# Attention and two feed-forward stages on one core: an order written by a planner gets new ranks and new costs

## The chip, the core and the metric

The program runs on one core of one Trainium2 chip. The metric is the time in microseconds (us) of an execution on the device; lower is better.

## What is computed

The reference, cut to what matters:

```python
def phi(x):                                   # x: (4, 8, 576, 64)
    proj = einsum('bhsd,df->bhsf', x, w_phi)  # 64 -> 128 features
    proj = proj - max(abs(proj), axis=-1)
    return concatenate([exp(proj), exp(-proj)], axis=-1)
q_p, k_p = phi(q), phi(k)
kv = einsum('bhsf,bhsd->bhfd', k_p, v);  z = sum(k_p, axis=2)
attn = einsum('bhsf,bhfd->bhsd', q_p, kv) / (einsum('bhsf,bhf->bhs', q_p, z) + 1e-6)
x = heads side by side                        # (2304, 512)
x = max(x @ w1, x @ w2, x @ w3) @ w_out       # 512 -> 768 -> 512
xn = x / sqrt(mean(x * x) + 1e-6) * rms_g
out = (silu(xn @ w_gate) * (xn @ w_val)) @ w_out2   # 512 -> 1536 -> 512
```

## The kernel before

**Three stages.** Attention is done in eight units of two heads; a unit has 1152 columns, taken in three thirds of 384 columns. The first feed-forward stage and the second one go over five column tiles (384, 512, 512, 512 and 384 of the 2304 columns), six times and six times. A product of the feed-forward stages is three matmuls, since each operand is held as a rounded part and a rest.

**One third of attention.** On the k side: `k_proj` (TensorE, tile `pk`), `k_max` and `k_sub` (VectorE, tiles `mk` and `e`), two exponentials per head (ScalarE, `e`), `kv_sum` (TensorE, `pkv`), and once per unit a copy `kvs` (ScalarE). On the q side: `q_proj` (TensorE, `pq`), two copies `pc` (ScalarE), `q_max` (GpSimd, a partition all-reduce into `mq`), `q_sub` (VectorE, `pc`), two exponentials (ScalarE, `eq` and `pc`), `attend` (TensorE, `nd`), then on VectorE `guard`, `invert` (both `den`) and `divide` (`xs`), the transposes `turn` (TensorE, again in a `pq` bank), and the rounded part `xh` (ScalarE) and the rest `xl` (VectorE) of the columns for the next stage. The denominators come from columns of ones beside v in the tiles `vt` and `vm`.

**The weights.** A piece of weights (512 columns of a 64-bit load) is turned into a rounded part and a rest by one ScalarE magnitude, five VectorE steps (`narrow`, L622, L626, L630, L634 and L636), a ScalarE rounding and two subtractions or additions (L650 and L652). These two run on VectorE for the first four pieces, which are prepared while attention runs, and on GpSimd for all later ones. The first 384 and the next 512 columns of the first feed-forward stage (tile `first`) are multiplied while attention ends.

**What sets the order.** Nothing in the program is ordered by loops: every step is an entry of a `Planner` (a step's engine, its rank, its assumed time, what it reads and writes). `order()` plays the program with these assumed times, and takes on each engine, of the steps that could start within 0.12 us of the first, the one with the lowest rank. The engines then run their instructions in that order. The assumed times are constants (`act_us`, `dve_us`, `pool_us`, `HALF`, `KPROJ`, `ISSUE`, `LOAD`), `U` is the assumed length of a unit, and `A` the rank at which the first feed-forward stage begins. Buffers are rings of slots: a new tenant of a slot waits until the last step of the old one is done. The rings that matter below are in PSUM: `pk` has banks 0 and 1, `pq` has 2, 3 and 7, the results `po` of the feed-forward stages have 4 to 7, and the sums and the spread scale of the normalisation (`pn`, L786 and L793) have bank 7 as well. All loads and stores are issued by SyncE's queue, in the planner's order. Ahead of everything TensorE runs ten matmuls on ones (`wake`, L342).

Of the kernel before, what the change touches and what calls it, by code (L numbers as in the profile page):

```python
# [46 lines left out]
class Planner:  # L47
# [18 lines left out]
    LAG = {"PE": 0.25, "DVE": 0.2, "ACT": 0.15, "POOL": 0.1}  # L66

    def op(self, eng, rank, busy, fn, r=(), w=(), lag=None, size=0, after=(), kind=None, when=0.0):
        lag = self.LAG.get(eng, 0.0) if lag is None else lag
        self.ops.append(dict(eng=eng, rank=rank, busy=busy, fn=fn, r=tuple(r), w=tuple(w), lag=lag, size=size,  # L70
                             after=after, kind=kind, when=when, i=len(self.ops)))

    def order(self):
# [39 lines left out]
        cand = {}  # L113
# [30 lines left out]
        while done < len(ops):  # L144
            best = None
            for eng, c in cand.items():
                e0 = free.get(eng, 0.0)
                l = []
                for i in c:
                    p = place(ops[i])  # L150
                    if p is not None:
                        l.append((max(e0, ready[i], p[0]), i, p[1]))
                if l:
                    first = min(x[0] for x in l)
                    pick = min((x for x in l if x[0] <= first + 0.12), key=lambda x: (ops[x[1]]["rank"], x[1]))
# [4 lines left out]
            t, i, claims = best  # L160
# [13 lines left out]
            if o["size"]:  # L174
                dma_free = max(dma_free, t + 1.2) + o["size"] / 240e3
# [16 lines left out]
def act_us(n, psum=False):  # L192
    return n / 1200.0 + (0.06 if psum else 0.105)


def dve_us(n):
    return n / 960.0 + 0.075


def pool_us(n):  # L200
    return n * 0.00235 + 0.15


R384, R256, R512, FULL, HALF, KPROJ = 0.173, 0.118, 0.229, 0.222, 0.13, 1.1
ISSUE = 0.6
# [3 lines left out]
def attn_moe_kernel(ctx, tc, qT, kT, vv, w_phi, w1, w2, w3, wo1, wg, wv, wo2, rms_g, out):  # L209
# [108 lines left out]
    def load_phi():  # L318
        for r in halves:
            nc.sync.dma_start(out=wst[r, :], in_=w_phi)  # L320
# [11 lines left out]
    def fill_v(i):  # L332
        vt, vm = vts[i]
        nc.gpsimd.memset(vm, 0.0)
        for b in range(2):
            nc.gpsimd.memset(vm[b * D:(b + 1) * D, :, b, D:D + 1], 1.0)
        nc.gpsimd.memset(vt[:, :, :, D:D + 1], 1.0)

    pl.op("SP", -100, 2 * ISSUE, load_phi, w=["wphi"], size=1 << 16, lag=2.0)
    def wake():  # L340
        for _ in range(10):
# [3 lines left out]
    pl.op("PE", -101, 4.0, wake, r=["ones2"], w=[new("nd", "wake")])  # L345
    pl.op("DVE", -99, 0.3, clear, w=["ones", "eps"])
    pl.op("ACT", -98, 1.4, lambda: nc.scalar.activation(out=eps, in_=eps, func=ACTF.Copy), r=["eps"], w=["eps"])
    for i in range(2):
# [5 lines left out]
          w=["gsc"], size=1 << 14, lag=4.0)  # L354
# [10 lines left out]
    U = 17  # L365
    LOAD = 2.5

    def unit(n):
# [9 lines left out]
        def load_v(b):  # L378
            if b < 2:
                r = halves[b]  # L380
                nc.sync.dma_start(out=vm[r, :, b, 0:D], in_=vv[g, hp, r, MIX])
# [525 lines left out]
```

## Time and profile before

| | us |
|---|---|
| median of 3 runs | 895.05 |
| lowest and highest run | 894.75 and 895.14 |
| the profiled execution's own time | 894.96 |
| its span, first to last instruction | 893.3 |
| TensorE busy in the span | 881.5 |
| VectorE busy | 572.8 |
| ScalarE busy | 335.5 |
| GpSimd busy | 242.3 |

The profiled execution is 0.09 us below the median, and 1.7 us of its time lie outside the span. TensorE's busy time counts a matmul until its modelled end, so that pipelined matmuls overlap; what a stage costs is read from when the next group of matmuls starts.

### The profile page before, as it was taken

How to read it: one execution, taken by the hardware profiler on the slowest of the kernel's cores; microseconds unless marked ns; L12 is line 12 of the kernel's file. 1: busy time of each engine (PE TensorE's matmuls, PEld its weight loads, DVE VectorE, ACT ScalarE, POOL GpSimd, SP SyncE). 2: the span in 40 equal slices, each digit the busy share in tenths (PEclk: the TensorE clock that was granted, in tenths of full speed). 3: DMA queues.
4: the chain of work that ended last, by engine and by line, in shares of the span. 5: the costliest groups of instructions: out<-in, count | busy, mean ns of one | idle time of the engine just before them, and what ended most of it. 6: DMA issues, size and time to landing. Idle time of an engine off the chain costs nothing.

```text
span 893.3 us, 15539 instructions
## 1 busy us (share of the span) xinstructions
PE 881.5 (99%) x6434; PEld 766.8 (86%) x6434; DVE 572.8 (64%) x1004; ACT 335.5 (38%) x640; POOL 242.3 (27%) x161
## 2 busy tenths in 40 slices
PE   8998999999999999999999999999999999999998
PEld 7887888898989889898978888898898888889887
DVE  4799897678775859496887337367366555533323
ACT  5998995452212212124565432123123122211110
POOL 3455453353312312043441222024024022200000
PEclk9999999999999999999999999999999999999999
DMA  8544321232220302011011013012011101000112
GB/s 213 139 121 125 106 73 44 72 95 70 72 72 1 95 25 72 23 48 48 1 48 48 1 48 94 1 48 71 24 47 48 48 8 41 1 0 1 48 59 106
DMA packets 53973, 51.38 MB, mean 58 GB/s; under 512 B 21520, under 2 KB 49296, under 8 KB 53904
## 3 DMA queue, kind: packets, MB, share of 16 engines
q1 hardware_dynamic: 53904, 50.41, 18.8%
q8 instruction: 50, 0.82, 0.4%
q14 instruction: 19, 0.16, 0.1%
HBM read 45.68 MB, written 4.72 MB: 56 GB/s over the span
## 4 chain that ended last, share of the span: by engine, by line
PE 89%; DVE 4%; POOL 3%; issue 2%; ACT 1%; POOLq 0%; ACTq 0%
PE up L361 56%; PE po L361 25%; POOL mq L474 3%; PE nd L499 2%; PE first L361 2%; PE pkv L432 1%; PE pq L468 1%; DVE pc L481 1%; PE pk L400 1%; DVE mk L407 1%; PE nd L342 1%; DVE xs L510 0%; PE pn L786 0%; PE pq L518 0%; PE pkv L429 0%
## 5 line engine op out<-in xcount | busy, mean ns | idle before, releaser
L361 PE MATMUL up<-xh,wp 128*128 128x512 f32 (+1 forms) x1632 | 488.5, 368 | 0.0
L361 PEld LDWEIGHTS up<-xh,wp 128*128 128x128 f32 x1632 | 302.6, 188 | 39.5
L361 PE MATMUL up<-xl,wp 128*128 128x512 f32 (+1 forms) x816 | 300.2, 368 | 0.0
L650 POOL TENSOR_TENSOR wa<-wa,wp 128x512 f32<-128x512 f32 x56 | 78.0, 1393 | 396.7 <-ACT wp L644 313.6
L361 PEld LDWEIGHTS up<-xl,wp 128*128 128x128 f32 x816 | 153.2, 188 | 20.4
L725 ACT CAST hh<-hf 128x512 fp32r<-128x512 f32 (+1 forms) x90 | 52.2, 580 | 246.6 <-DVE hf L833 130.8
L833 DVE TENSOR_TENSOR hf<-up,hf 128x512 f32<-128x512 f32 (+1 forms) x60 | 38.1, 635 | 161.4 <-PE up L361 159.0
L694 DVE TENSOR_TENSOR acc<-po,acc 128x512 f32<-128x512 f32 (+1 forms) x190 | 122.8, 659 | 21.0 <-PE po L361 19.3
L361 PE MATMUL po<-wp,hh 128*128 128x512 f32 x432 | 133.5, 390 | 0.0
L361 PEld LDWEIGHTS po<-wp,hh 128*128 128x128 f32 x432 | 80.7, 188 | 15.8
L831 ACT ACTIVATE hf<-up 128x512 f32<-128x512 f32 (+1 forms) x60 | 33.4, 556 | 160.5 <-PE up L361 160.5
L474 POOL PARTITION_ALL_REDUCE mq<-pc x24 | 66.9, 2788 | 68.1 <-ACT pc L471 62.4
L361 PE MATMUL po<-wp,hl 128*128 128x512 f32 x216 | 84.5, 391 | 0.0
L652 POOL TENSOR_TENSOR wp<-wa,wm 128x512 fp32r<-128x512 f32 x56 | 78.5, 1401 | 9.0 <-DVE wm L636 5.0
L361 PE MATMUL po<-hh,wp 128*128 128x512 f32 (+1 forms) x240 | 79.1, 370 | 1.6 <-DVE acc L800 1.6
L726 DVE TENSOR_TENSOR hl<-hf,hh 128x512 fp32r<-128x512 f32 (+1 forms) x90 | 67.1, 746 | 15.7 <-ACT hh L725 15.6
L749 DVE TENSOR_TENSOR hf<-up,hf 128x512 f32<-128x512 f32 (+1 forms) x56 | 35.6, 635 | 62.0 <-PE up L361 62.0
L636 DVE SCALAR_TENSOR_TENSOR wm<-wst,wm 128x512 f32<-128x512 uint32 x60 | 54.4, 906 | 1.0
L361 PEld LDWEIGHTS po<-hh,wp 128*128 128x128 f32 x240 | 44.7, 188 | 7.9 <-issue 1.9
L419 ACT ACTIVATE e<-e 128x384 f32<-128x384 f32 x96 | 47.0, 535 | 8.7 <-DVE e L412 8.1
L615 ACT ACTIVATE wm<-wst 128x512 f32<-128x512 f32 x60 | 40.1, 671 | 22.9 <-POOL wp L652 18.0
L622 DVE TENSOR_SCALAR wm<-wm 128x512 f32<-128x512 f32 x60 | 32.5, 543 | 24.5 <-ACT wm L615 24.5
(74 smaller groups left out, 948.2 us busy)
## 6 DMA issues: line engine op xcount, KB each, us to landing
wst<-in_moe_w_dram SPq DMA_DIRECT2D x18, 512.0 KB, 3.5
wst<-in_moe_w_out_dram SPq DMA_DIRECT2D x18, 512.0 KB, 3.5
wst<-in_moe_w_gate_dram SPq DMA_DIRECT2D x12, 512.0 KB, 3.5
wst<-in_moe_w_val_dram SPq DMA_DIRECT2D x12, 512.0 KB, 3.5
kraw<-in_kT_dram SPq DMA_DIRECT2D x24, 192.0 KB, 3.4
qraw<-in_qT_dram SPq DMA_DIRECT2D x24, 192.0 KB, 2.6
out_dram<-acc SPq DMA_DIRECT2D x18, 256.0 KB, 2.0
vt<-in_vv_dram SPq DMA_DIRECT2D x16, 256.0 KB, 4.0
```

Of the source, the lines that this page charges most:

```text
L361: mm(out=ps, lhsT=a, rhs=b, start=start and i == 0, stop=stop and i == n - 1)
L419: nc.scalar.activation(out=dst, in_=src, func=ACTF.Exp, scale=-1.0 if u else 1.0)
L474: nc.gpsimd.partition_all_reduce(buf(f"mq{n}.{c}").rearrange("p a c -> p (a c)"), buf(f"pc{n}.{c}").rearrange("p a c -> p (a c)"), P, bass ...
L615: nc.scalar.activation(out=buf(f"wm{self.id}").bitcast(FP32), in_=self.view()[1].bitcast(FP32), func=ACTF.Abs)
L636: nc.vector.scalar_tensor_tensor(out=mf, in0=lo.bitcast(U32), scalar=2.0 ** -52, in1=mf, op0=ALU.mult, op1=ALU.mult)
L650: eng.tensor_tensor(out=a, in0=a, in1=r32(buf(self.h)), op=ALU.subtract)
L652: eng.tensor_tensor(out=buf(self.l), in0=a, in1=buf(f"wm{self.id}").bitcast(FP32), op=ALU.add)
L694: nc.vector.tensor_tensor(out=acc, in0=p, in1=acc, op=ALU.add)
L725: pl.op("ACT", rank, act_us(n), lambda: nc.scalar.copy(out=buf(h)[:, 0:n], in_=buf(f)[:, 0:n]), r=[f], w=[h])
L726: pl.op("DVE", rank + 0.6, dve_us(n) + 0.1, lambda: nc.vector.tensor_tensor(out=buf(l)[:, 0:n], in0=buf(f)[:, 0:n], in1=r32(buf(h)[:, 0:n] ...
L749: pl.op("DVE", b_at(m, t, q), dve_us(n), lambda f=f, p=p, n=n: nc.vector.tensor_tensor(out=buf(f)[:, 0:n], in0=buf(p)[:, 0:n], in1=buf(f)[ ...
L833: pl.op("DVE", g_at(m, t, q + 4.1), dve_us(n), lambda f=f, p=ups[1], n=n: nc.vector.tensor_tensor(out=buf(f)[:, 0:n], in0=buf(p)[:, 0:n], ...
```

## The change

The planner is given other assumed times; it counts a switch of TensorE between matmuls on half the rows, on half the columns and on the whole array (`form`, 0.13 us); and it holds back a step of VectorE or GpSimd that reads two operands from SBUF, or is one of the simple `narrow` steps, while the other engine holds the port that the two share (`lock`, `fast`). All ranks get other constants. No matmul is added or taken away but four of the ten ahead of everything. `w_phi` is loaded from ScalarE's queue, and SyncE's first loads get an order of their own (`FIRST`). v gets its ones in the first and last column of a row of 130, so that a load writes 128 elements in one piece where it wrote twice 64. The matmuls of v have the same shapes as before. The core of the diff:

```diff
-    def op(self, eng, rank, busy, fn, r=(), w=(), lag=None, size=0, after=(), kind=None, when=0.0):
+    LAG = {"PE": 0.24, "DVE": 0.12, "ACT": 0.14, "POOL": 0.09}
+    TURN = 0.13
+    def op(self, eng, rank, busy, fn, r=(), w=(), lag=None, size=0, after=(), kind=None, when=0.0, form="whole", lock=0.0, fast=0.0):
...
-                        l.append((max(e0, ready[i], p[0]), i, p[1]))
+                        t = max(e0, ready[i], p[0])
+                        if ops[i]["lock"]:
+                            lo, hi, far = held["POOL" if eng == "DVE" else "DVE"]
+                            hi = far if ops[i]["fast"] else hi
+                            t = hi if lo <= t < hi else t
+                        late = eng == "PE" and form != ops[i]["form"]
+                        l.append((t, i, p[1], t + 0.0 * late))
...
+            if o["lock"]:
+                held[o["eng"]] = (t, t + o["lock"], t + max(o["lock"], o["fast"]))
...
+            if o["eng"] == "PE" and form != o["form"]:
+                busy += self.TURN
+                form = o["form"]
...
-            pools["attnk"].tile([P, NST - 1, 2, D + 1], FP32, name=f"vt{i}"),
-            pools["attnk"].tile([P, 2, 2, D + 1], FP32, name=f"vm{i}"),
+            pools["attnk"].tile([P, NST - 1, 2 * D + 2], FP32, name=f"vt{i}"),
+            pools["attnk"].tile([P, 2, 2 * D + 2], FP32, name=f"vm{i}"),
...
-            nc.sync.dma_start(out=wst[r, :], in_=w_phi)
+            nc.scalar.dma_start(out=wst[r, :], in_=w_phi)
...
-        for _ in range(10):
+        for _ in range(6):
             mm(out=buf("wake")[:, 0:P], lhsT=ones2, rhs=ones2, start=True, stop=True)
...
-    U = 17
-    LOAD = 2.5
+    U = 16.67
+    LOAD = 0.4
+    FIRST = {b: i - 40.0 for i, b in enumerate(("k1", "k0", "k2", "q0", "q1", "v2", "v3", "v0", "v1"))}
+    FIRST["q2"] = 8.58
...
-            pl.op("POOL", rk - 8, 2.75, lambda c=c: q_max(c), r=[f"{pc}:0", f"{pc}:1"],
+            pl.op("POOL", rk - 7.67, 2.69, lambda c=c: q_max(c), lock=1.57, fast=2.62, r=[f"{pc}:0", f"{pc}:1"],
...
-    A = NU * U + 24.0
+    A = NU * U + 16.39
```

What the new plan makes of it, at three places. First SyncE's queue at the program's start: `kraw`, `qraw`, `vt` and `vm` are the raw k, q and v of a third, `wst` is `w_phi`. Before:

```order
L320 DMA wst_84<-in_w_phi_dram 64x128 x2
L376 DMA kraw_124<-in_kT_dram 128x384
L376 DMA kraw_127<-in_kT_dram 128x384
L376 DMA kraw_129<-in_kT_dram 128x384
L385 DMA vt0_91<-in_vv_dram 128x8x64
L381 DMA vm0_92<-in_vv_dram 64x2x64
L385 DMA vt0_91<-in_vv_dram 128x8x64
L464 DMA qraw_134<-in_qT_dram 128x384
```

After:

```order
L391 DMA kraw_117<-in_kT_dram 128x384
L391 DMA kraw_122<-in_kT_dram 128x384
L391 DMA kraw_125<-in_kT_dram 128x384
L480 DMA qraw_127<-in_qT_dram 128x384
L480 DMA qraw_129<-in_qT_dram 128x384
L400 DMA vt0_91<-in_vv_dram 128x4x128 x2
L396 DMA vm0_92<-in_vv_dram 64x128 x2
```

The two loads of `w_phi` have left this queue, and two thirds of q stand ahead of v; the k of the first third is now the second load.

Second, TensorE at the program's start, with the ten or six matmuls on ones first, then `k_proj` (`pk`), `q_proj` (`pq`) and `kv_sum` (`pkv`). Before, up to the first `kv_sum`:

```order
L342 MATMUL nd<-ones_90 128x128 x10
L400 MATMUL pk<-wst,kraw 128x128 x12
L432 MATMUL pkv<-vt_91,e_162 64x65 x2
L432 MATMUL pkv<-vt_91,e_156 64x65 x2
```

After:

```order
L354 MATMUL nd<-ones_90 128x128 x6
L415 MATMUL pk<-wst,kraw 128x128 x6
L484 MATMUL pq<-qraw,wst 128x384 x4
L415 MATMUL pk<-wst,kraw 128x128 x6
L448 MATMUL pkv<-vt_91,e_161 64x65 x2
L448 MATMUL pkv<-vt_91,e_153 64x65 x2
```

Two thirds of `q_proj` have moved ahead of the second `k_proj`; before, a `q_proj` stood behind the first `kv_sum` and ahead of the third `k_proj`, and there none stands now.

Third, VectorE where weight steps lie between the `q_sub` of a third (written to `pc`) and its `divide` (`xs`). Before, of the second piece (L626, L630, L634):

```order
L529 TENSOR_TENSOR xl_612<-pq,xh_609 128x192 x2
L626 TENSOR_SCALAR wm<-wm 128x512
L630 SCALAR_TENSOR_TENSOR wa<-wst,wm 128x512
L481 TENSOR_TENSOR pc<-pc,mq 128x768
L502 TENSOR_SCALAR den<-nd 128x6
L634 TENSOR_SCALAR wm<-wa 128x512
L507 RECIPROCAL den<-den 128x6
L407 TENSOR_REDUCE mk<-pk 128x3
L510 TENSOR_TENSOR xs<-nd,den 128x384
```

After, of the second piece as well (L645, L649 and L653 are the same three steps):

```order
L645 TENSOR_SCALAR wm<-wm 128x512
L518 TENSOR_SCALAR den<-nd 128x6
L497 TENSOR_TENSOR pc<-pc,mq 128x768
L523 RECIPROCAL den<-den 128x6
L649 SCALAR_TENSOR_TENSOR wa<-wst,wm 128x512
L526 TENSOR_TENSOR xs<-nd,den 128x384
```

The step that wrote `wa` has moved from ahead of the `q_sub` to behind it, and the third of the steps into the next third, right behind that third's `q_sub` and `guard`; only one step is left between a `guard` and its `divide`.

## Rows read from the trace of the kernel before

**Rows 1.** The page's first part: busy us, share of span, instructions.

```profile
PE 881.5 (99%) x6434; PEld 766.8 (86%) x6434; DVE 572.8 (64%) x1004; ACT 335.5 (38%) x640; POOL 242.3 (27%) x161
```

**Rows 2.** The chain that ended last, in order of time: start us, us, what.

```profile
206.23 5.48 PE up L361 x24
255.77 5.48 PE up L361 x24
...
528.02 5.44 PE up L361 x24
...
602.01 5.44 PE up L361 x24
```

**Rows 3.** The chain in attention: first and twentieth attend, three q_proj in a row.

```profile
23.22 1.42 PE nd L499 x48
...
116.53 0.84 PE pq L468 x4
...
121.47 0.84 PE pq L468 x4
...
125.28 1.55 PE nd L499 x48
126.83 0.84 PE pq L468 x4
```

**Rows 4.** TensorE's waits: total us, times, longest.

```profile
PE pq L518 <- DVE xs L510: 3.0, 3, 2.2
PE po L361 <- DVE acc L800: 1.6, 1, 1.6
```

**Rows 5.** Timeline of VectorE, then of GpSimd, 79 to 87 us.

```profile
80.86 1.36 DVE L626 TENSOR_SCALAR wm<-wm 128x512 int32<-128x512 int32 x1
...
82.86 0.95 DVE L481 TENSOR_TENSOR pc<-pc,mq 128x768 f32<-128x768 f32 x1
...
83.80 1.83 DVE L634 TENSOR_SCALAR wm<-wa 128x512 int32<-128x512 int32 x1
...
86.08 0.54 DVE L510 TENSOR_TENSOR xs<-nd,den 128x384 f32<-128x384 f32 x1
...
79.20 2.74 POOL L474 PARTITION_ALL_REDUCE mq<-pc  x1 [2.50 <-ACT pc L471]
83.34 3.25 POOL L474 PARTITION_ALL_REDUCE mq<-pc  x1 [1.40 <-ACT pc L471]
```

**Rows 6.** Stretches of 1 us: length, busy us by engine, granted clock, DMA.

```profile
10.00:11.00 1.00, 1.00 (x21) 1.00 (x22) 1.00 (x3) 0.31 (x1) 0.03 (x1) 0.50 0.80 253
...
88.00:89.00 1.00, 1.00 (x23) 1.00 (x20) 1.00 (x3) 0.95 (x3) 0.00 (x0) 0.50 0.06 16
```

**Rows 7.** The chain right behind the stall at 84 to 87 us.

```profile
87.08 2.12 PE nd L499 x48
89.20 1.58 PE pq L468 x4
90.78 0.95 PE pk L400 x12
```

**Rows 8.** The chain at the start, and one later kv_sum.

```profile
1.11 4.63 PE nd L342 x20
5.74 1.02 PE pk L400 x12
6.76 1.57 issue
8.33 0.46 PE pk L400 x2
...
10.01 2.80 PE pkv L432 x48
12.81 0.85 PE pq L468 x4
13.66 0.67 PE pk L400 x12
...
118.04 1.55 PE pkv L432 x48
```

**Rows 9.** SyncE's first k loads in the timeline; time to landing, 0 to 6 us.

```profile
2.04 1.53 SPq L376 DMA_DIRECT2D kraw<-in_kT_dram  x3
...
kraw<-in_kT_dram SPq DMA_DIRECT2D x3, 192.0 KB, 2.6
```

**Rows 10.** Timeline around the change of stage: TensorE and VectorE.

```profile
441.95 0.65 PE L793 MATMUL pn<-ident,rc 128*128 128x128 f32 x4
...
447.52 0.75 DVE L800 SCALAR_TENSOR_TENSOR acc<-acc,gsc,pn 128x512 f32<-128x512 f32 x1
...
448.42 0.47 PE L361 MATMUL po<-hh,wp 128*128 128x512 f32 x1 [1.65 <-DVE acc L800]
```

**Rows 11.** One normal step of each of two kinds, VectorE, 96 to 117 us.

```profile
107.33 0.39 DVE L622 TENSOR_SCALAR wm<-wm 128x512 f32<-128x512 f32 x1
...
112.62 0.65 DVE L630 SCALAR_TENSOR_TENSOR wa<-wst,wm 128x512 int32<-128x512 int32 x1
```

More of the change, by code (lines that the diff above doesn't have):

```diff
@@ L65 @@
     SWAP = 7.4
-    LAG = {"PE": 0.25, "DVE": 0.2, "ACT": 0.15, "POOL": 0.1}
-    def op(self, eng, rank, busy, fn, r=(), w=(), lag=None, size=0, after=(), kind=None, when=0.0):
+    LAG = {"PE": 0.24, "DVE": 0.12, "ACT": 0.14, "POOL": 0.09}
+    TURN = 0.13
+    def op(self, eng, rank, busy, fn, r=(), w=(), lag=None, size=0, after=(), kind=None, when=0.0, form="whole", lock=0.0, fast=0.0):
         lag = self.LAG.get(eng, 0.0) if lag is None else lag
         self.ops.append(dict(eng=eng, rank=rank, busy=busy, fn=fn, r=tuple(r), w=tuple(w), lag=lag, size=size,
-                             after=after, kind=kind, when=when, i=len(self.ops)))
+                             after=after, kind=kind, when=when, form=form, lock=lock, fast=fast, i=len(self.ops)))
     def order(self):
@@ L353, in attn_moe_kernel @@
     pl.op("SP", 20, ISSUE, lambda: nc.sync.dma_start(out=gsc, in_=rms_g.rearrange("(k p) -> p k", p=P)),
-          w=["gsc"], size=1 << 14, lag=4.0)
+          w=["gsc"], size=1 << 14, lag=4.0, when=60.0)
     def mm3(ps, terms, start=True, stop=True):
@@ L380, in load_v @@
                 r = halves[b]
-                nc.sync.dma_start(out=vm[r, :, b, 0:D], in_=vv[g, hp, r, MIX])
+                nc.sync.dma_start(out=vm[r, b, 1:2 * D + 1], in_=vv[g, hp, r, MIX].rearrange("p j d -> p (j d)"))
             else:
@@ L426, in kv_sum @@
                     first, last = t == 0 and u == 0, t == NST - 1 and u == 1
+                    head = slice(j * (D + 1), (j + 1) * (D + 1))
                     for r in halves:
                         if t == MIX:
-                            mm(out=ps[r, u], lhsT=e[:, r], rhs=vm[:, j], start=first, stop=last)
+                            mm(out=ps[r, u], lhsT=e[:, r], rhs=vm[:, :, head], start=first, stop=last)
                         else:
                             b = int(t > MIX)
-                            mm(out=ps[r, u, b, :], lhsT=e[:, r], rhs=vt[:, t - b, j, :], start=first, stop=last)
+                            mm(out=ps[r, u, b, :], lhsT=e[:, r], rhs=vt[:, t - b, head], start=first, stop=last)
         def kv_copy(j):
@@ L554, in unit @@
             for j in range(2):
-                pl.op("PE", rk + j, 6 * HALF, lambda c=c, j=j: attend(c, j),
+                pl.op("PE", rk - 0.47 + 0.57 * j, 6 * HALF, lambda c=c, j=j: attend(c, j), form="cols",
                       r=[eq, f"{pc}:0", f"{pc}:1", f"kvs{n}.{j}"], w=[f"{nd}:{j}"])
-            pl.op("DVE", rk + 2.0, 0.12, lambda c=c: guard(c), r=[f"{nd}:0", f"{nd}:1"], w=[den])
-            pl.op("DVE", rk + 2.1, 0.14, lambda c=c: invert(c), w=[den])
-            pl.op("DVE", rk + 2.2, dve_us(C), lambda c=c: divide(c), r=[f"{nd}:0", f"{nd}:1", den], w=[xs])
-            pl.op("PE", rk + 2.5, 0.3, lambda c=c: turn(c), r=["ident", xs], w=xt)
+            pl.op("DVE", rk + 2.76, 0.085, lambda c=c: guard(c), r=[f"{nd}:0", f"{nd}:1"], w=[den])
+            pl.op("DVE", rk + 2.76 + 0.1, 0.1, lambda c=c: invert(c), w=[den])
+            pl.op("DVE", rk + 2.76 + 0.2, dve_us(C), lambda c=c: divide(c), r=[f"{nd}:0", f"{nd}:1", den], w=[xs])
+            pl.op("PE", rk + 2.54, 0.16, lambda c=c: turn(c), form="rows", r=["ident", xs], w=xt)
             for h, part in [(h, part) for h in range(2) for part in parts(c, h)]:
@@ L663, in plan @@
             new("wp", self.l)
-            pl.op("SP", w, ISSUE, self.load, w=[st], size=P * 512 * 8, lag=LOAD, when=max(0.0, w - 20) if i < 4 else 0.0)
+            pl.op("SP", w, ISSUE, self.load, w=[st], size=P * 512 * 8, lag=LOAD, when=max(0.0, w - 20.0) if i < 4 else 0.0)
             if self.wide:
@@ L718, in fn @@
             mm3(buf(ps)[:, 0:CW[t]], [(wh[:, k * P:(k + 1) * P], wl[:, k * P:(k + 1) * P], h[:, k, :], l[:, k, :]) for k in range(KD)])
-        pl.op("PE", rank, 12 * mm_us(CW[t]), fn, r=xin(s, t) + [piece.h, piece.l], w=[ps], lag=0.3, when=EARLY)
+        pl.op("PE", rank, 12 * mm_us(CW[t]), fn, r=xin(s, t) + [piece.h, piece.l], w=[ps], lag=0.2, when=EARLY)
         return ps
@@ L743, in attn_moe_kernel @@
             early = "first" if m == 0 and C0[t] + n <= T else "up"
-            ups = [plan_up(b_at(m, t, q), 0, f"{key}.{i}", pieces1[m][i], t, early) for i, q in enumerate((0.0, 1.97, 4.92))]
+            ups = [plan_up(b_at(m, t, q), 0, f"{key}.{i}", pieces1[m][i], t, early) for i, q in enumerate((0.0, 0.31, 4.41))]
             f = new("hf", f"hf{key}")
```

126 lines of the change are left out of this document (65 added, 61 removed).

## Prediction

> **What bounds the kernel now.** I read the page's busy times first, then the chain of work that ended last, then TensorE's waits, and last the timeline where these waits lie. TensorE is busy for 99% of the span [rows 1], so the time is TensorE's work plus the stretches in which it waits or runs slowly. The chain shows that the two feed-forward stages hold no such stretch: one of the six rounds of the first stage takes 255.77 - 206.23 = 49.54 us, and one round of the second 602.01 - 528.02 = 73.99 us [rows 2]. Six of each are 297.2 + 443.9 = 741.1 us, and they are the same matmuls after the change. The other 893.3 - 741.1 = 152.2 us are the start, attention, the change of stage and the tail, and only there can time be won.
>
> In attention the reader is to see how dense TensorE is. Where nothing waits, a third takes 121.47 - 116.53 = 4.94 us, and the third of a unit that holds the mixed tile takes 126.83 - 121.47 = 5.36 us [rows 3]. From the first `attend` at 23.22 to the twentieth at 125.28 us there are 19 thirds, of which 6 are of the longer kind: dense they would be 13 x 4.94 + 6 x 5.36 = 96.4 us, and they took 102.1 us. So 5.7 us of this stretch are excess, and everything ahead of 23.22 us is the filling of the pipeline. The last thirds are filled up with `first` matmuls and show no wait.
>
> The waits name the places: TensorE waited three times for `xs` before `turn`, at the longest 2.2 us, and once 1.6 us in the feed-forward part for the scaled `acc` [rows 4]. The long one lies at 84 to 87 us. There the step L626 took 1.36 us, of which most went by until the all-reduce of 79.20 had ended at 81.94; `q_sub` could start only at 82.86; then L634, standing between `guard` and `invert`, took 1.83 us beside the next all-reduce, which began at 83.34, and so `divide` ended at 86.62 [rows 5]. A step of this shape takes 0.39 us when it has the port [rows 11]. Behind the stall TensorE's granted clock was 0.50 [rows 6], its lower level of 1.2 GHz: the next `attend`, `q_proj` and `k_proj` took 2.12, 1.58 and 0.95 us [rows 7], against 1.55, 0.84 [rows 3] and 0.67 [rows 8]. That is 0.57 + 0.74 + 0.28 = 1.6 us more. So one stall of this kind costs 2.2 + 1.6 = 3.8 us, two thirds of the excess.
>
> **The change, term by term.**
>
> *The start.* TensorE's first `k_proj` begins at 5.74 us, right when the ten matmuls on ones end; these take 4.63 us [rows 8]. Six take 0.6 of it and end near 3.9 us. SyncE issued the first k load at 2.04 us, with 0.5 us an issue, and it landed 2.6 us later [rows 9], so it was there before TensorE was. With `w_phi` on another queue SyncE starts with k, about 1.2 us earlier; the k that is needed is the second load now, so it lands near 2.04 - 1.2 + 0.5 + 2.6 = 3.9 us too. The first `k_proj` comes some 1.6 us earlier. Then the order differs. Before, the second `k_proj` waited until 8.33 for a free bank of `pk`; the first `kv_sum` followed at 10.01 and took 2.80 us at a granted clock of 0.50 [rows 6, 8], where 1.55 is usual; a `q_proj` of 0.85 us came next, and the third `k_proj` ran only at 13.66. After, four matmuls of `q_proj` fill the wait for the bank (1.7 us, or 3.2 us at the lower clock), and none stands ahead of the third `k_proj`: 0.85 us less, and 1.25 us less if the clock is up for `kv_sum`. The second `k_proj` then gains 0 to 1.5 us and the third 0.9 to 3. Since the first two `q_max` are begun early, `q_sub` is no longer what the first `attend` waits for; it inherits the gain of the k side. Bounds: 0 and -4 us; I take the middle of the third `k_proj`'s gain and the earlier q side, **-2.5 us**.
>
> *The thirds between.* Removed is the pattern of 84 to 87 us: the second piece's L630 stands behind `q_sub` and not ahead of it, and L634 is put into the next third, directly behind `q_sub` and `guard`, when an all-reduce has just ended. Steps ahead of `q_sub` still meet the all-reduce, but `q_sub` waits for that same all-reduce anyway, so they cost only their own 0.39 to 0.65 us [rows 11]. What stands between `guard` and `divide` is one such step, and TensorE has a `q_proj`, a `k_proj` and half a `kv_sum` (0.84 + 0.67 + 0.78 = 2.3 us) to do before `turn` asks for `xs`. Without the stall 5.7 - 3.8 = 1.9 us of excess stay, and I leave 0.2 for new small waits. Bounds: everything goes (-5.7), or a stall like it arises elsewhere (0). I take **-3.6 us**.
>
> *The change of stage.* The 1.65 us wait is one for a bank: a `po` result of bank 7 had to wait until VectorE had read the spread scale of L793 from that bank for the last time, 447.52 + 0.75 us, though the transposes were done at 442.6 [rows 10]. The new order again puts some 5 us of matmuls between such a transpose and the next use of bank 7, twice, where the need was 5.8 us. Bounds 0 and -1.65 us; I take **-0.4 us**.
>
> *Costed at nothing.* The new ranks of the feed-forward stages: the matmuls are the same, and a round has no wait to lose [rows 2]. Were a step late there, it would come back in every round. ScalarE's two issues of `w_phi`: it has nothing to do before the first `k_sub`, which follows the first `k_proj`; without this cover, 1.2 us. The layout of v: its loads go in fewer, longer pieces, which helps only the start, and is inside that term's bounds; matmuls, `guard` and `divide` keep their sizes. The last thirds: the order of `q_proj`, `first` and `attend` differs a little, and TensorE has 72 `first` matmuls to put into gaps as before.
>
> The sum is -2.5 - 3.6 - 0.4 = -6.5 us on the profiled execution's own 894.96 us: 888.5 us. The median of the runs is 0.09 us above that execution, so I forecast **888.5 us**.
>
> **Two rules beside the rows.** The row shows a granted clock of 0.50 in the stretch from 10 us on, after TensorE had waited from 6.76 on [rows 6, 8]. The Trainium skill, "TensorE: Matmul & The Clock Gate", Part 1 (What's actually happening), has it that the throttled state is the default and that activity releases it. This speaks against shortening the matmuls on ones, and is the first rival below. For the port, [rows 5] show L626 ending only after the all-reduce. The Trainium skill, "SBUF — State Buffer", section Who interferes with whom, says that the second to ask for the shared port blocks fully, and that issue order decides who that is. The trace agrees at L626, and this is why the second and third rival are about order.
>
> **The rivals.**
>
> *Cold start (14%).* Six matmuls on ones don't bring the clock up, and the first `q_proj`, `k_proj` and `kv_sum` run at the lower level: 2 x 0.74 + 0.28 + 1.25 = 3.0 us more, by the rows at either level. That eats the start's 2.5 us: 894.96 - 4.0 = 891.0. For it: before, ten were needed and even so the clock fell at 10 us. Against: `q_proj` now fills the hole.
>
> *A stall again (14%, two of them 6%).* The planner's account of the port is not the chip's, and one of the four pieces prepared during attention meets the all-reduce between `guard` and `divide`: 3.8 us, 892.3 us. For it: GpSimd's all-reduces come when ScalarE's copies are done, and a drift of 1 us, as at 83.34 where one began 1.4 us after the last, is enough. Two such stalls give 896.1, about no change.
>
> *Slower (7%).* The same mechanism in three or all of the four pieces: 11.4 to 15.2 us of stalls against the gains of 6.5 us, so 899.9 to 903.7. It decides from the third stall on. Against it: before, with four pieces and no account of the port at all, there was one.
>
> *Denser (9%).* The start gives 4 us, all excess and the bank's wait go: -4 - 5.7 - 1.65 = -11.4 us, 883.6.
>
> **How the numbers follow.** The forecast has 50%, with 886 to 890.5 of its own. The range from 883.5 to 894 takes in the denser case, the cold start and one stall, and leaves out two or more stalls. Less than 0.2% (1.8 us) can't be told from no change in this kernel. Faster: 50 + 14 + 14 + 9 = 87%; same: the two stalls, 6%; slower: 7%.
>
> **What would show it.** Right: the first `attend` near 20.7 us; no wait for `xs` over 1 us; no granted clock of 0.50 between 15 and 150 us; the twentieth `attend` near 119 us; rounds of 49.5 and 74.0 us as before. The forecast is wrong if the first `attend` stays near 23 us, if a wait of 2 us for `xs` appears beside an all-reduce, or if the rounds get longer.

## The result, and the profile after

The kernel after takes **885.39 us** (median of 4 runs, 884.6 to 886.44) against 895.1 us before (894.75 to 895.26, on the same chip): a ratio of 0.9903, 95% interval 0.9887 to 0.992. The profiled execution took 886.07 us, with a span of 884.4 us; before it was 894.96 and 893.3, so both are 8.9 us shorter. Of 46 executions of the kernel before that were timed in all, five took 891.0 to 891.5 us at a mean granted clock of 0.998 or 0.999 and the others 893.2 to 895.6 us (0.996 to 0.998 where it is on record); its median differs by 1 us from one measurement to the next (894.1 to 895.1).

The page's first part after answers to [rows 1]:

```profile
PE 878.5 (99%) x6426; PEld 764.6 (86%) x6426; DVE 550.6 (62%) x1004; ACT 337.1 (38%) x642; POOL 238.2 (27%) x161
```

VectorE runs the same 1004 instructions in 22.2 us less. That is not less work: the time is gone from weight steps and rests that the planner now holds back (the step that was L626, for one, fell from a mean of 689 to 549 ns), while steps that have no `lock`, such as the sums of `acc`, keep their means (659 ns). TensorE's waits after (us in total, times, longest), to be held against [rows 4]:

```profile
PE pk L415 <- DMA wst<-in_w_phi_dram: 0.6, 1, 0.6
PE pkv L448 <- ACT e L434: 0.2, 1, 0.2
PE pn L806 <- POOL sq L800: 0.2, 1, 0.2
```

No wait for `xs` and none for `acc` is left. Beside these, TensorE waits 1.1 us for the ones in the program's first microsecond, as before. The chain of work that ended last, in order of time (start us, us, what), answers to [rows 2, 3, 8]:

```profile
10.51 1.55 PE pkv L448 x48
...
21.36 1.43 PE nd L515 x48
...
118.84 1.40 PE nd L515 x48
...
198.79 5.48 PE up L373 x24
...
248.35 5.48 PE up L373 x24
...
525.93 5.44 PE up L373 x24
...
599.93 5.44 PE up L373 x24
```

Cut at the same places as in the prediction, the two kernels compare so (in us; the third line ends at the first `up` of the first feed-forward stage, 156.53 in the trace before and 149.06 after):

| stretch | before | after | change | forecast |
|---|---|---|---|---|
| start to first `attend` | 23.22 | 21.36 | -1.9 | -2.5 |
| first to twentieth `attend` | 102.06 | 97.48 | -4.6 | -3.6 |
| twentieth `attend` to first `up` | 31.25 | 30.22 | -1.0 | 0 |
| one round of the first stage | 49.54 | 49.56 | 0 | 0 |
| wait at the change of stage | 1.65 | 0.2 | -1.5 | -0.4 |
| one round of the second stage | 73.99 | 74.00 | 0 | 0 |

The first `attend` comes 1.9 us earlier, the second line is 4.6 us shorter and the change of stage has lost its wait. The lines sum to -9.0 us, which is the span's 8.9 to rounding.

What went on between `guard` and `divide` at the old stall, in VectorE's timeline after (to be held against [rows 5]):

```profile
83.15 0.95 DVE L497 TENSOR_TENSOR pc<-pc,mq 128x768 f32<-128x768 f32 x1
84.02 0.16 DVE L518 TENSOR_SCALAR den<-nd 128x6 f32<-128x6 f32 x1
84.09 0.42 DVE L653 TENSOR_SCALAR wm<-wa 128x512 int32<-128x512 int32 x1
84.43 0.18 DVE L523 RECIPROCAL den<-den 128x6 f32<-128x6 f32 x1
84.64 0.56 DVE L526 TENSOR_TENSOR xs<-nd,den 128x384 f32<-128x384 f32 x1
```

This is the step that took 1.83 us before, in the same gap between `guard` and `invert`, and it takes 0.42 us because the next all-reduce begins only at 85.19. The step didn't have to leave the gap; it had to be there when the port was free.

### The profile page after: what moved, and what is told of

It reads as the page before. It is cut to its first block, busy times and chain, and to the rows that moved or that the text cites. A ratio compares the mean times of both kernels' runs of the same rounds, so it can differ in the third digit from the quotient of the medians.

```text
span 884.4 us, 15529 instructions
## 1 busy us (share of the span) xinstructions
PE 878.5 (99%) x6426; PEld 764.6 (86%) x6426; DVE 550.6 (62%) x1004; ACT 337.1 (38%) x642; POOL 238.2 (27%) x161
## 2 busy tenths in 40 slices
DMA packets 44757, 51.38 MB, mean 58 GB/s; under 512 B 3088, under 2 KB 40080, under 8 KB 44688
## 4 chain that ended last, share of the span: by engine, by line
PE 96%; ACT 2%; DVE 1%; DMA 0%; POOL 0%; issue 0%; ACTq 0%; POOLq 0%
PE up L373 56%; PE po L373 25%; PE nd L515 4%; PE pkv L448 3%; PE pq L484 2%; PE pk L415 2%; PE first L373 2%; PE pq L535 1%; PE pkv L445 1%; DMA wst<-in_w_phi_dram 0%; PE pn L806 0%; ACT e L434 0%; DVE xl L825 0%; POOL sq L799 0%; ACT eq L501 0%; ACT pc L501 0%
## 5 line engine op out<-in xcount | busy, mean ns | idle before, releaser
L671 POOL TENSOR_TENSOR wp<-wa,wm 128x512 fp32r<-128x512 f32 x56 | 76.6, 1370 | 9.2 <-DVE wm L655 5.0
L746 DVE TENSOR_TENSOR hl<-hf,hh 128x512 fp32r<-128x512 f32 (+1 forms) x90 | 61.8, 688 | 16.0 <-ACT hh L745 15.3
L634 ACT ACTIVATE wm<-wst 128x512 f32<-128x512 f32 x60 | 40.2, 672 | 44.6 <-POOL wp L671 19.3
L655 DVE SCALAR_TENSOR_TENSOR wm<-wst,wm 128x512 f32<-128x512 uint32 x60 | 47.6, 798 | 0.6
L373 PEld LDWEIGHTS po<-wp,hl 128*128 128x128 f32 x216 | 40.5, 188 | 8.5
```

The lines of the kernel that those rows point to most:

```text
L373: mm(out=ps, lhsT=a, rhs=b, start=start and i == 0, stop=stop and i == n - 1)
L634: nc.scalar.activation(out=buf(f"wm{self.id}").bitcast(FP32), in_=self.view()[1].bitcast(FP32), func=ACTF.Abs)
L655: nc.vector.scalar_tensor_tensor(out=mf, in0=lo.bitcast(U32), scalar=2.0 ** -52, in1=mf, op0=ALU.mult, op1=ALU.mult)
L671: eng.tensor_tensor(out=buf(self.l), in0=a, in1=buf(f"wm{self.id}").bitcast(FP32), op=ALU.add)
L746: pl.op("DVE", rank + 0.6, dve_us(n), lambda: nc.vector.tensor_tensor(out=buf(l)[:, 0:n], in0=buf(f)[:, 0:n], in1=r32(buf(h)[:, 0:n]), op= ...
```

## The experiments

Twelve kernels ran, each beside the kernel before on the same chip, whose median was then 894.1 to 894.83 us. Where one of them is set against the kernel after, that is a difference of medians from two measurements, which need not be on one chip.

### The stall by itself

In the kernel before, one step of the second piece is taken from its place between `guard` and `invert` and put right behind that third's `divide`:

```diff
-        return [ops[i]["fn"] for _, i in sorted(seq)]
+        out = [ops[i] for _, i in sorted(seq)]
+        step = [o for o in out if o["eng"] == "DVE" and "wm1" in o["w"]][3]
+        at = out.index(step)
+        to = next(n for n in range(at, len(out)) if any(k.startswith("xs") for k in out[n]["w"]))
+        out.insert(to, out.pop(at))
+        return [o["fn"] for o in out]
```

> The kernel before with one instruction moved: the second piece's L634 goes from between guard and invert to right behind that third's divide. Theory (one step that is blocked at the shared port costs a wait of 2.2 us and 1.6 us at the lower clock): divide ends near 84.9 instead of 86.6 us, at most 0.5 us of the wait is left and the granted clock stays at 1.00, so 3 to 3.5 us less, about 891.8 us. Rival (VectorE is behind there anyway, the wait comes back in the next third): 1 us less or nothing, 894 to 895 us.

It took 892.07 us (891.61 to 892.37), ratio 0.9972 [0.9962, 0.9982]. TensorE's waits in it:

```profile
PE po L366 <- DVE acc L805: 1.7, 1, 1.7
...
PE pq L523 <- DVE xs L515: 1.6, 4, 0.6
```

The wait of 2.2 us is gone and the one at the change of stage has stayed. One entry of the order was worth 2.8 us, a little less than the theory's 3 to 3.5, and the rival falls. The prediction priced a stall of this kind at 3.8 us. That price can be read at the place itself, from the twelfth `attend` to the fourteenth. Before and after:

```profile
79.85 0.29 PE L499 MATMUL nd<-kvs,eq 128*64 128x65 f32 x4
...
94.02 0.28 PE L499 MATMUL nd<-kvs,eq 128*64 128x65 f32 x4
```

```profile
76.68 0.29 PE L515 MATMUL nd<-kvs,eq 128*64 128x65 f32 x4
...
87.03 0.28 PE L515 MATMUL nd<-kvs,eq 128*64 128x65 f32 x4
```

These two thirds took 14.17 us before and 10.35 us after, so 3.8 us went here, as priced. With the one step moved they take 11.43 us (79.97 to 91.40).

### The account of the port, and the ranks

First the kernel after without the account: its ranks, costs and start stay.

```diff
-                        if ops[i]["lock"]:
+                        if False:
```

> The changed kernel with the same ranks and costs, but its planner no longer holds a step back for the shared port. Theory (it is the account of the port that keeps the weight steps clear of the all-reduces): at least one wait for xs of more than 1 us comes back in attention, 2 to 4 us more, 887.5 to 889.5 us. Rival (the new ranks and costs alone spread the weight steps): within 1 us of the changed kernel's 885.4 us.

It took **903.68 us** (902.65 to 905.77), ratio 1.0106 [1.0093, 1.0119]: 18.3 us more than the kernel after, and slower than the kernel before. Both expectations fell in size. In attention the theory came near in size but not in place: the first `up` begins at 152.29 us, 3.2 us later than in the kernel after, and nearly all of that is lost behind the nineteenth `attend` (112.44 us, where the kernel after has 112.22), in a wait for `eq` and not for `xs`. The thirds before it lose 0.5 us from the second `attend` on; the first `attend` comes 1.6 us earlier (19.64), which the second gives back but for 0.3 us. The rest of the loss lies in the feed-forward stages, where neither expectation had it. Its longest waits:

```profile
PE pn L806 <- POOL sq L800: 3.1, 2, 1.6
PE po L373 <- ACT hh L745: 3.0, 3, 2.2
PE po L373 <- DVE hl L746: 2.2, 4, 0.9
PE pq L535 <- ACT eq L501: 1.7, 1, 1.7
```

Three of the four are waits of the feed-forward stages. Two more kernels take one half of the account away each. Without that of the all-reduces:

```diff
-lambda c=c: q_max(c), lock=1.57, fast=2.62, r=[f"{pc}:0", f"{pc}:1"],
+lambda c=c: q_max(c), r=[f"{pc}:0", f"{pc}:1"],
```

> The kernel after, but the planner takes GpSimd's all-reduces as holding no port (the account of the weight steps and sums stays); ranks and costs of after. With the whole account ignored the time was 903.68 us, and 3.2 us of the loss lay ahead of the second feed-forward tile, the rest in the feed-forward stages. Theory (two separate losses, and the larger one is that of GpSimd's weight steps against VectorE's narrow steps): here only the first one comes back, 887 to 889.5 us, with the feed-forward rounds free of waits. Rival (the small loss in the last thirds puts everything behind it out of step): most of the 18 us comes back, 897 to 904 us.

It took 889.14 us (889.14 to 889.67), ratio 0.9948 [0.9929, 0.9966]: 3.75 us above the kernel after, as the theory had it. The loss lies in the last thirds: the first `up` begins at 152.16 us, 3.1 us later. There two weight steps stand ahead of a `q_sub` and beside an all-reduce:

```profile
130.58 2.92 POOL L490 PARTITION_ALL_REDUCE mq<-pc  x1 [3.82 <-ACT pc L487]
...
131.08 1.45 DVE L641 TENSOR_SCALAR wm<-wm 128x512 f32<-128x512 f32 x1 [1.91 <-ACT wm L634]
132.57 1.21 DVE L645 TENSOR_SCALAR wm<-wm 128x512 int32<-128x512 int32 x1
```

In the kernel after these two steps take 0.42 and 0.41 us, at 131.62 and 133.88 us, when the all-reduce begun at 128.92 has run its 2.74 us. The `q_sub` behind them is late, through it `eq`, and TensorE waits 1.7 us for that. And without that of GpSimd's weight steps (both calls) and sums of squares:

```diff
-kind="plain" if eng == "POOL" else None, lock=us)
+kind="plain" if eng == "POOL" else None, lock=us * (eng != "POOL"))
...
-sum_tiles, w=[sq], kind="plain", lock=pool_us(2 * n) + pool_us(n))
+sum_tiles, w=[sq], kind="plain")
```

> The kernel after, but the planner takes GpSimd's weight subtractions and sums as holding no port, and keeps the account of the all-reduces; VectorE's order in attention is that of after up to the last thirds. Theory (two separate losses): most of the 18.3 us comes back, 897 to 902 us, as waits of TensorE for hh, hl and acc in the first feed-forward stage, beside VectorE weight steps of over 0.9 us, and the twentieth attend stays near 118.7 us. Rival (out of step from the last thirds on): 885 to 888 us.

It took 899.41 us (897.43 to 901.73), ratio 1.0062 [1.0039, 1.0085]: 14.0 us above. The two halves, 3.75 + 14.0 = 17.8, make up the 18.3 us, so these are two separate losses, and the rival by which a small shift in attention brings the whole falls. What one such place in the feed-forward stage looks like, in the timeline of the last kernel:

```profile
185.28 1.36 POOL L671 TENSOR_TENSOR wp<-wa,wm 128x512 fp32r<-128x512 f32 x1
...
185.52 1.40 DVE L645 TENSOR_SCALAR wm<-wm 128x512 int32<-128x512 int32 x1
...
187.56 0.55 DVE L746 TENSOR_TENSOR hl<-hf,hh 128x384 fp32r<-128x384 f32 x1
...
188.17 0.44 PE L373 MATMUL po<-hl,wp 128*128 128x384 f32 x1 [1.57 <-DVE hl L746]
```

GpSimd's step begins first; VectorE's L645, begun 0.24 us later, takes 1.40 us, and ends 0.28 us after GpSimd's has. The split `hl` behind it on VectorE is late, and TensorE, which needs it for the way down, waits 1.57 us. This kernel's waits in the feed-forward stages:

```profile
PE po L373 <- DVE hl L746: 4.2, 4, 1.7
PE pn L806 <- POOL sq L800: 3.1, 2, 1.6
PE po L373 <- ACT hh L745: 1.5, 1, 1.5
...
PE po L373 <- DVE acc L820: 0.4, 1, 0.4
PE pn L806 <- DVE acc L820: 0.4, 1, 0.4
```

They are nine waits and sum to 9.6 us. In the ten microseconds from 410 on, behind one of them, the granted clock was 0.83, another 1.7 us. The remaining 2.6 of the 13.9 us by which its span is longer I can't assign to rows.

Then the other way round: the kernel before with the account alone (`lock` and `fast` on the same steps, with the values of the change where these are numbers of their own; a `lock` that is a step's assumed time follows the old formula), and its own ranks, assumed times, loads and v.

```diff
+                        t = max(e0, ready[i], p[0])
+                        if ops[i]["lock"]:
+                            lo, hi, far = held["POOL" if eng == "DVE" else "DVE"]
+                            hi = far if ops[i]["fast"] else hi
+                            t = hi if lo <= t < hi else t
```

> The kernel before with the account of the port alone (lock and fast); its ranks, assumed times, loads and v stay. Theory (the account takes away what it is meant to): the stall of 2.2 us for xs at 84 to 87 us goes and the lower clock behind it, so about 3.8 us less, 891 to 892 us; the start and the wait of 1.6 us for bank 7 stay. Rival (account and ranks belong together, as the kernel after without the account shows): with ranks set for other costs a stall comes up in another place, 894 to 898 us.

It took **889.34 us** (888.38 to 890.29) against 894.1, ratio 0.9949 [0.9932, 0.9967]. The rival falls: the account works with ranks that were set without it. The theory undershot, since it brought 4.8 us and not 3.8 or less: the wait for bank 7 went too. What the account does is best read from the weight steps on VectorE while attention runs (23 to 150 us; after the bar busy us and the mean ns of one). Before:

```profile
L626 DVE TENSOR_SCALAR wm<-wm 128x512 int32<-128x512 int32 x5 | 4.5, 893 | 0.0
L634 DVE TENSOR_SCALAR wm<-wa 128x512 int32<-128x512 int32 x4 | 4.1, 1023 | 0.0
```

The kernel before with the account alone, where these are L633 and L641:

```profile
L641 DVE TENSOR_SCALAR wm<-wa 128x512 int32<-128x512 int32 x5 | 2.1, 422 | 0.0
L633 DVE TENSOR_SCALAR wm<-wm 128x512 int32<-128x512 int32 x5 | 2.0, 400 | 0.0
```

And the kernel after:

```profile
L645 DVE TENSOR_SCALAR wm<-wm 128x512 int32<-128x512 int32 x6 | 4.2, 706 | 0.0
L653 DVE TENSOR_SCALAR wm<-wa 128x512 int32<-128x512 int32 x6 | 3.0, 493 | 0.1
```

With the account alone these two kinds take about what they take alone (0.39 us for a step of this shape, [rows 11]). Not every step does: the first step of a piece, L622 before and L629 here, went from a mean of 406 to 514 ns. In the kernel after some still run beside an all-reduce, one of 0.94 us at 77.39 among them, at a place where nothing waits for it.

### The start

The kernel before with the start of the change alone: `w_phi` on ScalarE's queue, the order `FIRST`, six matmuls on ones.

```diff
-            nc.sync.dma_start(out=wst[r, :], in_=w_phi)
+            nc.scalar.dma_start(out=wst[r, :], in_=w_phi)
...
-        for _ in range(10):
+        for _ in range(6):
...
-            lk = base + 2.0 * c - 32 if n < 2 else rk
+            lk = FIRST[f"k{c}"] if n == 0 else base + 2.0 * c - 32 if n < 2 else rk
```

> The kernel before with the new start alone: w_phi on ScalarE's queue, the new order of the first loads, six matmuls on ones. Theory (what the start saves is carried to the end, since TensorE is dense behind it): the first attend some 2 us earlier and the whole 1.5 to 2.5 us shorter, about 893 us, with the stall near 84 us still there. Rival (the earlier start is given back before the feed-forward stage, as VectorE and the stall set the pace): first attend earlier, the whole within 0.5 us of 895.1 us.

It took 893.41 us (891.55 to 894.64), ratio 0.9983 [0.9975, 0.9991], 1.4 us less, between theory and rival. The waits of 2.2 us for `xs` and 1.6 us for `acc` are still there. The span of the profiled execution is 1.2 us shorter, and yet the trace speaks for the rival: the first `attend` begins 1.1 us earlier in the timeline (21.95 against 23.05 us), but the third `attend` and the thirteenth begin when they did before (32.71 and 87.00):

```profile
32.76 0.29 PE L502 MATMUL nd<-kvs,eq 128*64 128x65 f32 x4
...
87.04 0.34 PE L502 MATMUL nd<-kvs,eq 128*64 128x65 f32 x4
...
92.46 0.29 PE L502 MATMUL nd<-kvs,eq 128*64 128x65 f32 x4
```

So the earlier start is given back by the third `attend`. What this execution gains comes behind the stall: the granted clock from 88 to 91 us was 1.00, where it was 0.50 in the trace before, and from the thirteenth `attend` to the fourteenth it took 5.42 us instead of 7.02. Nor did the start itself come as forecast, since the first `kv_sum` took 2.87 us here as it did before.

The start together with the account, on the kernel before:

> The kernel before with the account of the port and the start (w_phi on ScalarE's queue, the new order of first loads, six matmuls on ones) but its own ranks and assumed times. The account alone gave 889.34 us against 894.1, the start alone 893.41 against 894.8. Theory (the two gains lie in different places and add): 887.5 to 888.5 us; what is left to 885.4 us is the ranks' and costs' own part, 2 to 3 us. Rival (the ranks give nothing of their own once account and start are there): 885 to 886 us. Second rival (the new start shifts attention so that a stall comes up): 890 to 892 us.

It took 887.63 us (887.19 to 889.02), ratio 0.9936 [0.992, 0.9953]: 1.7 us less than with the account alone. Here the earlier start does reach the end: the first `attend` begins at 19.92 us, where it is 21.68 with the account alone, and the first `up` at 147.60 instead of 149.60. So the start is worth something once the account has taken the stalls away; the two add as the theory had it, and 2.2 us are left for the new ranks and assumed times (1.4 us between the profiled executions, 887.48 and 886.07).

The rest of the kernels of the start vary the kernel after. Ten matmuls on ones:

```diff
-        for _ in range(6):
+        for _ in range(10):
```

> The changed kernel with ten matmuls on ones again and the same order otherwise. Theory (the changed kernel's first k_proj waits for w_phi until 5.36 us anyway, and its first 9.35 us run at the lower clock): the ten matmuls end when the data is there, the clock comes up earlier, 0.5 to 1.5 us less, 884 to 885 us. Rival (VectorE and the banks of pk set the pace of the start, the clock does not matter): within 0.3 us, 885.4 us. Second rival (they end too late and push k_proj back): 0.3 us or more longer.

It took 884.95 us (884.7 to 885.51), ratio 0.9895 [0.9882, 0.9907], with the first `attend` at 20.89 us in the timeline, where after has 21.19 and two kernels with its start have 21.59 (the one without the account of the weight steps) and 20.97 (one with older offsets, further below). That is too small a difference to be told from the kernel after; so taking out the four matmuls gave nothing that can be told.

Both loads of `w_phi` back on SyncE's queue, ahead of k:

```diff
-            nc.scalar.dma_start(out=wst[r, :], in_=w_phi)
+            nc.sync.dma_start(out=wst[r, :], in_=w_phi)
```

> The kernel after with both loads of w_phi back on SyncE's queue, ahead of k; six matmuls on ones as in after. Theory (the gain at the start comes mostly from the order of the first steps, and the second queue gives little, since w_phi's second half landed only at 5.36 us): first attend at 21 to 22 us, 885 to 886.2 us, the wait of 0.6 us for w_phi gone and one for k of at most 1.5 us in its place. Rival (the second queue is the gain): first attend near 22.8 us, 886.8 to 887.5 us.

It took 888.06 us (887.38 to 888.56), ratio 0.9936 [0.9922, 0.995], 2.7 us more, with the first `attend` at 22.70 us in the timeline. The rival holds, with the time 0.6 us above its range: TensorE now waits 1.3 us for k and 1.4 us for q, both issued two loads later, and the granted clock was 0.80 from 6 to 9 us and 0.64 from 9 to 12. The second queue is worth what it keeps off these two loads. Then only the first half of `w_phi` on SyncE's queue, and the second alone on ScalarE's, so that both land early:

```diff
-        for r in halves:
-            nc.scalar.dma_start(out=wst[r, :], in_=w_phi)
+        for r, e in zip(halves, (nc.sync, nc.scalar)):
+            e.dma_start(out=wst[r, :], in_=w_phi)
```

> The kernel after with w_phi's first half at the head of SyncE's queue and its second half alone on ScalarE's; six matmuls on ones. Theory (the start fell 0.6 us short of the forecast because w_phi's second half landed at 5.36 us): the wait for w_phi goes or shrinks to 0.3 us, first attend at 20.5 to 20.8 us, 884.7 to 885.1 us. Rival (the lower clock until 9.35 us is what costs, and it stays): first attend at 21 to 21.3 us, 885.2 to 885.7 us.

It took 887.42 us (886.64 to 888.88), ratio 0.993 [0.9915, 0.9945]: 2.0 us *more*, where both expected no loss. Its waits, and two stretches of 3 us (busy us of TensorE, its weight loads, VectorE, ScalarE, GpSimd; then the granted clock):

```profile
PE pq L484 <- DMA qraw<-in_qT_dram: 1.5, 2, 1.3
...
PE pk L415 <- DMA kraw<-in_kT_dram: 0.7, 1, 0.7
```

```profile
9.00:12.00 3.00, 3.00 (x30) 2.71 (x28) 1.02 (x3) 2.15 (x6) 1.91 (x2) 0.50 1.03 300
12.00:15.00 3.00, 3.00 (x52) 2.88 (x48) 0.93 (x2) 1.98 (x4) 3.00 (x2) 0.58 0.94 260
```

The same stretch in the kernel after:

```profile
9.00:12.00 3.00, 3.00 (x64) 2.73 (x61) 1.67 (x4) 2.43 (x7) 1.48 (x2) 1.00 1.03 297
```

The wait for `w_phi` is gone, but TensorE now stands from 4.03 to 4.69 us for k and from 5.63 to 6.93 us for q, both of which were issued one load later; from 8 to 14 us the granted clock is at its lower level, and the first `attend` begins at 23.07 us in the timeline. In the kernel after TensorE waits once in these microseconds, 0.6 us, and then has work without a gap. So the wait for `w_phi` covered two others.

### v and the first feed-forward stage

The v of before in the kernel after (ones behind each head's 64 columns; `guard`, `divide` and the loads on the old views):

```diff
-            pools["attnk"].tile([P, NST - 1, 2 * D + 2], FP32, name=f"vt{i}"),
+            pools["attnk"].tile([P, NST - 1, 2, D + 1], FP32, name=f"vt{i}"),
...
-                nc.sync.dma_start(out=vt[:, t0:t0 + MIX, 1:2 * D + 1], in_=vv[g, hp, :, t0 + b:t0 + b + MIX].rearrange("p t j d -> p t (j d)"))
+                nc.sync.dma_start(out=vt[:, t0:t0 + MIX, :, 0:D], in_=vv[g, hp, :, t0 + b:t0 + b + MIX])
```

> The kernel after with the v of before: ones behind each head's 64 columns, loads that write twice 64 elements, guard and divide on the old views; every engine keeps the order of after. Theory (the layout of v was costed at nothing, its transfers are hidden): 885 to 886 us, first attend at 21 to 21.4 us, and only the count of packets under 512 B goes back to about 21500. Rival (the short packets delay the first loads of k, q and v): first attend 0.5 to 1 us later, 886 to 886.6 us.

It took 886.3 us (885.29 to 887.39), ratio 0.9916 [0.9901, 0.9931]. The median is 0.9 us above that of the kernel after and the intervals overlap, while its profiled execution of 885.29 us is the shorter of the two. The packets under 512 B went from 3088 back to 21521, and yet the first `attend` came no later (20.71 us in the timeline), which is against the rival. Inconclusive as to the whole: the layout's worth lies between nothing and about 1 us.

The old offsets inside a tile of the first feed-forward stage, in the kernel after:

```diff
-enumerate((0.0, 0.31, 4.41))]
+enumerate((0.0, 1.97, 4.92))]
...
-            h, l = plan_split(b_at(m, t, 6.95), key, n)
+            h, l = plan_split(b_at(m, t, 7.6), key, n)
...
-            for k, q in enumerate((4.06, 4.06 + 0.49, 7.05, 7.05 + 0.49)):
+            for k, q in enumerate((3.94, 4.43, 6.89, 7.38)):
...
-        plan_norm(t, b_at(N1 - 1, t + 1, 2.93))
+        plan_norm(t, b_at(N1 - 1, t + 1, 4.0))
```

> The kernel after with the offsets of before inside a tile of the first feed-forward stage (0, 1.97, 4.92 for the three products; 3.94, 4.43, 6.89, 7.38 for the way down; 7.6 for the split; 4.0 for the sums of squares). Theory (the wait for bank 7 at the change of stage went because of these offsets, which move the way down and the sums): a wait of 1 to 1.7 us for acc comes back, 886 to 887.5 us. Rival (it went because of the planner's other times and the account): no such wait, 885 to 885.8 us. If the rounds of the first stage get waits, the time is over 888 us.

It took 886.35 us (885.2 to 887.01), ratio 0.9914 [0.9898, 0.993]. One wait for `acc` came back:

```profile
PE pn L806 <- DVE acc L820: 0.7, 1, 0.7
```

It is shorter than the theory's 1 to 1.7 us and at another step; the time lies in the theory's range, but the median is within 1 us of the kernel after with overlapping intervals. The new offsets are not needed to take the 1.65 us away: the kernel before with the account alone has the old offsets and no such wait.

## Why the prediction came out right, point by point

**The frame held.** The time came from the start, attention and the change of stage, the rounds kept their 49.5 and 74.0 us, and TensorE stayed 99% busy. The forecast of 888.5 us had -6.5 us for what became -8.9 on the profiled execution. Of the signs that were to show it, the twentieth `attend` (118.84 us, forecast near 119), the waits for `xs`, the granted clock and the rounds came in; the first `attend` (21.36 us, forecast near 20.7) did not.

**The thirds between** (-3.6 forecast, -4.6 measured): the mechanism was as put, and the size off by one oversight. The 5.7 us of excess were counted against dense thirds that each hold a `q_proj`; the trace before has 18 of them between the first and the twentieth `attend` (72 tile matmuls), and the one after has 19 (76). With 0.84 us for the missing one [rows 3] the excess before was 6.5 us, and after it is 97.5 - 96.4 = 1.1. So 5.4 us of excess went. Of these, 3.8 us went at the stall, between the twelfth and the fourteenth `attend`, and that is the price the prediction gave; the single moved step brought 2.7 of them. The other 1.6 us I didn't separate place by place. The planner's account is the cause at the stall: with it alone these two thirds take 10.56 us (79.36 to 89.92), the blocked steps are gone and the time falls by 4.8 us.

**The last thirds** (0 forecast, -1.0 measured): this is that same `q_proj`, done earlier now. Three stand behind the twentieth `attend` before, two after.

**The start** (-2.5 forecast, -1.9 measured): "The first `k_proj` comes some 1.6 us earlier" failed as a step. Its first matmuls did begin at 3.98 us, but the others waited for `w_phi`'s second half, which landed only at 5.36 us:

```profile
5.36 1.43 PE L415 MATMUL pk<-wst,kraw 64*128 64x128 f32 x9 [0.61 <-DMA wst<-in_w_phi_dram]
```

I had looked at when k lands and not at `w_phi`, which now travels beside it. And the two thirds of `q_proj` took the longer of the two times I gave, from 6.38 to 9.84 us. What did come in full is the first `kv_sum`, 1.55 us instead of 2.80, and a chain in which no `q_proj` stands ahead of the third `k_proj`. The first rival, the cold start, occurred in part: by their durations the two thirds of `q_proj` ran at the lower level (the 2 x 0.74 us of that rival's 3.0), while the first `kv_sum` did not. How near the rest of it was is shown by the kernel with `w_phi` on two queues: loads that are issued one place later bring the lower clock back up to 14 us, and waits and clock together cost 1.9 us at the first `attend`. The matmuls on ones were not the point, since ten or six of them make no difference that can be told.

**The change of stage** (-0.4 forecast, -1.5 measured): the step that failed is the cause. I took it for a question of distance between two uses of a bank. The traces show something else. In the one before, the spread scale was in the bank at 442.6 us, yet VectorE began to read it at 444.95:

```profile
441.78 1.28 ACT L831 ACT_TABLE_LOAD   x1
...
443.46 1.21 ACT L615 ACTIVATE wm<-wst 128x512 f32<-128x512 f32 x2
444.14 0.43 DVE L622 TENSOR_SCALAR wm<-wm 128x512 f32<-128x512 f32 x1 [1.79 <-ACT wm L615]
```

VectorE stood idle for 1.79 us at a weight step that waited for ScalarE, and ScalarE was loading its table for the first `silu`, after standing idle itself for 3.85 us until 441.24, waiting for VectorE's `hf`; the readers of the bank were queued behind. A rest `xl` (446.92 us, 0.69) then stood ahead of the fourth reader [rows 10]. After the change they start as soon as the scale is there, and run in one go:

```profile
438.88 0.60 PE L813 MATMUL pn<-ident,rc 128*128 128x128 f32 x4
...
439.56 2.71 DVE L820 SCALAR_TENSOR_TENSOR acc<-acc,gsc,pn 128x512 f32<-128x512 f32 x4
```

That the weight step stands elsewhere is read from the traces; that it alone makes the difference was not tried by itself. The account alone took the wait away, the old offsets did not bring it back.

**Costed at nothing.** The feed-forward ranks cost nothing, as forecast, but my reason was wrong. The sentence "the matmuls are the same, and a round has no wait to lose" overlooks that a round can gain a wait: with these ranks and no account of GpSimd's weight steps the stages take 14 us more. Nor would a late step "come back in every round": that kernel has nine waits in the feed-forward stages, five of them from 177 to 212 us, in the first two rounds, and four from 412 to 481 us, around the change of stage; the rounds between have none. The rival *slower* priced the ranks without a good account at 899.9 to 903.7 us, and 903.68 us is what the kernel without the account takes; the number met, the place did not, since three of its four longest waits lie in the feed-forward stages, the fourth in the last thirds, and none between `guard` and `divide`. That the number met is luck.

**Which part brought what.** On the kernel before: the account alone -4.8 us, the start another -1.7, the ranks, assumed times and v -2.2. These sum to 8.7 us and not to 9.7, since the kernel before had other medians beside each. Without the account the start gave 1.4 us, and in its trace not by reaching the end. On the kernel after the same account is worth 18.3 us. The new ranks, costs and start without it are 8.9 us slower than the kernel before, so the ranks are not a gain of their own but one that the account makes possible. Which of the ranks and assumed times bring the last 2.2 us was not tried.

## What to carry to other kernels

Where two engines share a port, list the instructions whose mean time is well above their shortest one, and look at what stands behind them in the queue: the price of a blocked step is paid there. An order tuned with one model of the costs is worth little under another, so test the model and the order apart before crediting either. And before making a late load earlier, look at what its wait was covering. A gain at the start is not a gain of the whole until the trace shows it behind the next stall.

## What was not expected of the hardware

- A VectorE step that begins 0.24 us after a GpSimd step on the same port took 1.40 us where it takes 0.40 alone, and ended 0.28 us after the other. The Trainium skill, "SBUF — State Buffer", section Who interferes with whom, says that the second to ask blocks fully, and this row agrees. That such blocking lengthened the feed-forward stages by 14 us, while VectorE was busy for only 65% of the span, was the surprise.
- Between 6.8 and 9.5 us the kernel after needs 2.71 us for six matmuls of `q_proj`, 0.45 us each, where four take 0.84 us [rows 3]; by the durations this is the lower of the clock's two levels. The granted clock of the stretch reads 1.00, but the trace has no clock record before 9.35 us, and the view takes unrecorded time as 1.00; so it says nothing there, and the durations decide. With ten matmuls on ones the records begin at 6.86 us, at 1.00, and from 7.00 us on seven such matmuls took 1.96 us.
- `w_phi` at 32 KB a load took a median of 3.3 us from issue to landing on a queue of its own, while the three k loads of 192 KB issued beside it took 2.6 us; before, ahead of k on the same queue, it took 2.2 us.
